# One core, windowed attention and a mixture of experts: the output buffer of a token group as two tiles, with a new set of planner constants

## The chip, the core and the metric

The kernel runs on one core of a Trainium2 chip. The metric is the device time of one execution in microseconds (us). Engines are named as the profile names them: PE (TensorE, matrix products), PEld (its weight loads), DVE (VectorE), ACT (ScalarE), POOL (GpSimd) and SP (SyncE). POOL and SP issue most of the transfers here.

## What is computed

Sliding-window attention with a few sink keys, and then a mixture of four experts on its output. Cut to what matters:

```python
# q, k, v: 4 batches x 8 heads x 768 tokens x 64; n_sink 4, window 128
scores = q @ k.T / sqrt(64)
keep = (pos_k < 4) | ((pos_q - pos_k >= 0) & (pos_q - pos_k < 128))
a = softmax(where(keep, scores, -1e9))
x = (a @ v).transpose(0, 2, 1, 3).reshape(3072, 512)
p = domain_probs / domain_probs.sum(-1)          # 3072 x 4
out = sum(p[:, e:e+1] * (relu(x @ w1[e]) @ w2[e]) for e in range(4))   # w1 512 x 1024, w2 1024 x 512
```

## The kernel before, in words

**Groups and pairs.** Each batch b is cut into three groups g of 256 tokens. A *pair* (b, g) is one such group. Its output is 256 tokens x 512 columns in fp32, held as two halves of 128 tokens. The products of the experts for one pair and one expert are a *unit* (b, g, e).

**Attention.** Scores (L692) and sink scores (L653) go to PSUM, ACT takes the exponential (L717), DVE multiplies by the mask (L711, L726), PE multiplies with the values (L751 for the sinks, L758), DVE takes the reciprocal of the sums (L785), and ACT (L797; in batch 0 DVE, L788) scales into the tile onat. In batch 0, PE turns onat into xT (L816). In batches 1 to 3, a transposing transfer that SP issues does it (L775), and q and k are turned by transposing transfers too (L252, qkT<-qkn). The scores use 64 rows of the PE array at a time (two heads side by side), the sinks 32 columns.

**First layer.** For most units x @ w1 is formed with seven products of half-size blocks instead of eight (P1 to P7, L1158); sums of the token blocks are made on DVE before (L1127), sums of the weight blocks too (L380 to L386), and ACT and DVE combine the products (L1204, L1217, L1211, L1226) and apply Relu and gate (L1191). The other units take the plain product (L1071). The first product of a unit takes two PSUM banks; where the bank for P2 and P6 was not written over its whole width by its last user, one extra matmul of 512 columns (L1166) writes it once.

**Second layer.** For the first two groups of batch 0 it is plain (L1422, results added on DVE by L1432 and L1434 into a tile that both halves share). For the other ten pairs it is again seven products, now over all four experts at once (L1335), in the order of CHAIN: P1, P2, P6, P5, P7, P3, P4. The blocks of the output are C11 and C12 (first 128 tokens, left and right 256 columns) and C21 and C22 (last 128 tokens). After P1, ACT copies the sum to the other bank (L1375). P2 is copied to C11 by ACT, P6 to C12, P5 to C22 and P4 to C21 (all L1397). DVE adds P7 to C22 (L1386) and P3 to C12 (L1381). After P3 the first half is stored (L1383), after P4 and P7 the second (L1324), both by SP.

**The buffer.** Of the ten pairs, the last but one uses two tiles left over from attention. For the others, line 1363 takes one tile osb of both halves with a single buffer (bufs=1). The next tile of that name takes the same memory, and so the first write to it waits for every reader of the one before.

**What sets the order.** The kernel writes its instructions in an order that a planner in the same function decides. It keeps a modelled clock for each engine and picks at each turn what PE does next: a step of attention, a product of a first layer, a product of the second. Work for ACT and DVE is put in a list with a time when it is ready and a time when it is due (`later`), and taken from there by due time (`flush`). SP's and POOL's transfers are written as the planner reaches them. Each engine then works through its own instructions strictly in the order written. The constants at the top (L60 to L100) set due times, preferences and pace: SHARE_OF how much of the expert work of a batch passes while the attention of the next is done, MASK, GATE, GATE0, FORM and TOKEN the slack of DVE's tasks, LOW_PRODUCT and OPEN the rank of products and of opening another unit, HOLDS when two heads' scores are kept for one turn, CHORES how many sums of the second layer may wait at DVE.

Of the kernel before, what the change touches and what calls it, by code (L numbers as in the profile page):

```python
# [11 lines left out]
FP32 = mybir.dt.float32  # L12
# [4 lines left out]
def kernel(  # L17
# [17 lines left out]
    E, Dm, F = moe_w1.shape  # L35
    Ntok, Dout = out.shape

    P = 128
# [19 lines left out]
    ]  # L58

    NGATE = 4  # L60
    FIRST = 1
    START = {0: (1, 0), 1: (0, 2), 2: (0, 0), 3: (1, 0)}
    MIX = 6
    SHARE_OF = (0.9, 0.79, 0.98)
    LEAD = (1.01, 1.0)
    DUE = 1.9
    LOW_PRODUCT = 2.3
    LOW_SECOND = 2.7
    HIGH_PRODUCT = 1.9
    EARLY = -0.01  # L70
    MASK = 4000
    GATE = 1500
    GATE0 = 900
    FORM = 6000
    TOKEN = 5000
    MARGIN = 0
    HOLD = 0
    FULL = 7
    STEP0 = 0.01
    READY = 40  # L80
    WIDE = 2
    OPEN = 2.2
    SOON = 34000
    NEARLY = 2
    ROWED = 24000
    GATED = 38000
# [1 line left out]
    ROWS1 = 1500  # L88
    ONACT = 1
    ONE = 2  # L90
    HOLDS = 1
    MORE = 2
    BOTH = 1
    PAIR = 0
    OVER = 4
    ALONE = 1.3
    BEHIND = 1500
    CHORES = 3
    BIASED = 1
    FAST = tuple(START)  # L100
    BZ = 0
# [122 lines left out]
    mo = ctx.enter_context(tc.tile_pool(name="moe_sb", bufs=2))  # L224
# [224 lines left out]
    def load_gates():  # L449

        while len(gate_sb) < len(mix.order) and (
            len(gate_sb) < (NGATE if t["pe"] > GATED else FIRST) or mix.order[len(gate_sb) - NGATE] in mix.finished
        ):
# [3 lines left out]
    def load_gate(pair, e):  # L457

        x = mo.tile([P, 2, P], FP32, name="gates", tag="gates", bufs=NGATE)
        if FIRST <= len(gate_sb) < NGATE:  # L460
            nc.vector.memset(x[0:1, 0, 0:1], 0.0)
# [474 lines left out]
    out_sb = {}  # L936

    class Mixture:


        def __init__(self):
            self.early = {g: list(range(E)) for g in range(NEARLY)}
            self.open = []
            self.units = []
            for b, g in PAIRS:
                fast = [e for e in range(E) if self.is_fast(b, g, e)]
                slow = [e for e in range(E) if e not in fast]
                if b == 0:
                    fast, slow = list(range(E)), []
                while fast or slow:  # L950
                    for x in (fast, slow):
                        if x:
                            self.units.append((b, g, x.pop(0)))
            self.order = list(self.units)
            self.T, self.T_at, self.fast, self.finished = {}, {}, {}, set()
            self.second, self.live, self.since, self.turn, self.credit = [], 0, 0, 0, 0.0
            self.H, self.H_at, self.H_part = {}, {}, {}
            self.S, self.S_at, self.waiting, self.last = {}, {}, [], []
            self.products = [(b, g, m) for b, g in PAIRS for m in CHAIN]
            self.piece, self.part, self.chores = 0, 0, 0  # L960
            self.at, self.S4_at, self.C22 = {}, {}, {}
            self.done = 0.0
            self.stored, self.homed = [], False
            self.spare, self.lent = [], {}
# [170 lines left out]
        def emit_fast(self, u, m, ready):  # L1135
# [86 lines left out]
            elif m == "P2":  # L1222
                gated(H[:, 0, :, 1], y, 1, end, GATE, slots["Y"])
            elif m == "P7":
# [91 lines left out]
        def emit_product(self):  # L1316
            ready = self.product_ready()
            b, g, m = self.products[0]
            self.done += QF * G
            self.credit = max(self.credit - QF * G, 0.0)  # L1320
            r = (b * NQB + 2 * g) * P

            def store(at, c=slice(0, Dout)):
                nc.sync.dma_start(out=out[r + P:r + 2 * P, c], in_=out_sb[b, g][1][:, c])  # L1324
                sp(at)
            bank = self.bank(b, g, m)
            other = acc[1 - bank][:, 0:G]
            final = (b, g) == PAIRS[-1]
            x = acc[bank][:, 0:G]
            e, k = self.order_of(b, g)[self.piece], self.piece  # L1330
            split = final and m == CHAIN[-1]
            cs = slice(self.part * P, self.part * P + P) if split else slice(0, G)
            y = self.rest if split and self.part else x[:, cs]
            for f in range(QF):
                nc.tensor.matmul(  # L1335
                    y, lhsT=self.operand(b, g, e, m)[:, f], rhs=forms[e][m][:, f, cs],
                    start=(k == 0 and f == 0 and m in (("P1", "P5", "P2") if final else ("P1", "P5"))), stop=(k == E - 1 and f == QF - 1), skip_group_check=True,
                )
            end = pe(QF * (P if split else G), ready, n=QF)
            self.piece = (k + 1) % E  # L1340
            if split and k == E - 1:
                nc.scalar.copy(out=out_sb[b, g][1][:, cs], in_=y)
                store(act(P, end), cs)
                self.part += 1
            if split and self.part < 2:
                return
            if m == CHAIN[-1]:
                if (b, g, e) in self.lent:
                    self.spare.append(self.lent.pop((b, g, e)))
                else:  # L1350
                    self.live -= 1
            if k < E - 1:
                return
            self.products.pop(0)
            if split:
                return
            if m == "P1":
                late = not att.more() and ahead == B - 1
                if late and self.homed:
                    x2 = [sb.tile([P, 2, 4 * P], BF16, name="aT", tag="aT", bufs=4) for _ in range(2)]  # L1360
                    out_sb[b, g] = [i.rearrange("p h w -> p (h w)").bitcast(FP32) for i in x2]
                else:
                    x2 = mo.tile([P, 2, Dout], FP32, name="osb", tag="osb", bufs=1)
                    out_sb[b, g] = [x2[:, i] for i in range(2)]
                self.homed = late and not self.homed
                self.C22[b, g] = join(2, lambda at: store(at))
            o = out_sb[b, g]
            C11, C12, C21, C22 = o[0][:, 0:G], o[0][:, G:], o[1][:, 0:G], o[1][:, G:]
            acc_free[bank], seeded = 1e12, acc_free[1 - bank]
            if m == "P1" and not final:  # L1370
                acc_free[1 - bank] = 1e12

            def run(engine):
                if m == "P1" and not final:
                    nc.scalar.copy(out=other, in_=x)  # L1375
                    acc_free[0] = acc_free[1] = act(G, seeded)
                elif m == "P2" and final:
                    nc.vector.tensor_add(C11, C11, x)
                    acc_free[bank] = dve(G)
                elif m == "P3":  # L1380
                    nc.vector.tensor_add(C12, C12, x)  # L1381
                    acc_free[bank] = at = dve(G)
                    nc.sync.dma_start(out=out[r:r + P, :], in_=o[0])  # L1383
                    sp(at)
                elif m == "P7":
                    nc.vector.tensor_add(C22, C22, x)  # L1386
                    acc_free[bank] = at = dve(G)
                    if final:
                        store(at, slice(G, Dout))
                        i = min((i for i in range(6) if whole[i]), key=lambda i: ring[i])  # L1390
                        self.rest = psum.tile([P, P], FP32, name="rest", tag=f"r{i}", bufs=1)
                        nc.scalar.copy(out=self.rest, in_=x[:, P:G])
                        acc_free[bank] = act(P, end)
                    else:
                        self.C22[b, g](at)
                else:
                    nc.scalar.copy(out={"P1": C11, "P2": C11, "P6": C12, "P5": C22, "P4": C21}[m], in_=x)  # L1397
                    acc_free[bank] = at = act(G)
                    if m == "P4":
                        self.C22[b, g](at)  # L1400
            later("dve" if m in ("P3", "P7") or final and m == "P2" else "act", end, 200, run)
# [7 lines left out]
        def emit_second(self):  # L1409
            ready = self.second_ready()  # L1410
            g, s, e = self.second.pop(0)
            if g not in out_sb:
                out_sb[g] = mo.tile([P, 2, Dout], FP32, name="osb0", tag=f"wide{g}" if g < 2 else "osb", bufs=1)
                if g == 0:
                    gates()
            dst = out_sb[g][:, s]
# [40 lines left out]
    ahead, upto, loaded, wide, rowed = 0, 0.0, 0, 0, 0  # L1457
# [23 lines left out]
    while mix.more() or att.more():  # L1481
        now = t["pe"]

        if not att.more() and ahead == B - 1 and not wide:
            wide = 1
# [27 lines left out]
        if turns and (ahead < 2 or not mix.second) and landed.get(("qk", *turns[0]), 1e12) < now and (turns[0][0] <= ahead or turns[0][0] == ahead + 1 and not att.todo):  # L1513
            x = turns.pop(0)
            turn_nat(*x)
            b = x[0]
# [12 lines left out]
        if ahead + 1 < B and not att.more() and (ahead == 0 or (ahead + 1, 0) in turned_at) and (ahead == 0 or mix.done >= sum(work[:ahead]) * LEAD[ahead - 1]):  # L1529
            ahead += 1  # L1530
            att = Attention(ahead)
            upto = mix.done
        share = (sum(work[:ahead]) - upto) * SHARE_OF[max(ahead - 1, 0)]
        due = ahead == 0 or att.steps * share <= (mix.done - upto) * att.total
# [75 lines left out]
```

## Time and profile before

| | |
|---|---|
| median of 3 runs | 357.3 us (356.98 to 357.76) |
| the profiled execution | 357.25 us, of which the span, first to last instruction, is 355.5 |
| PE busy | 349.7 us, 98% |
| DVE busy | 305.9 us, 86% |
| ACT busy | 165.2 us, 46% |
| POOL busy | 73.6 us, 21% |
| mean granted PE clock | 0.998 |
| transfers | 37.80 MB, mean 106 GB/s |
| L1158, first layer by seven products | 2240 matmuls of 128 columns |
| L1335, second layer by seven products | 1120 matmuls, 1104 of them of 256 columns |

How to read it: a line of the page names engine, line of the kernel and operation, then output<-inputs. On PE, a matmul's row lasts from its start to the modelled end of its results, 219 ns for 128 columns, while the next matmul starts much earlier. So the busy share says when PE had something under way, and the distance between the starts of two matmuls says whether it worked at its full rate. Waits are written as "who waited <- for whom: us in total, times, longest". In a timeline each row is a start, a length and the instructions merged into it, with the idle time before it in brackets. In the table of stages, each engine has its busy time and its number of instructions.

### The profile page before, as it was taken

What the parts mean: (1) busy time and instruction counts of PE and PEld (TensorE: products, weight loads), DVE (VectorE), ACT (ScalarE), POOL (GpSimd) and SP (SyncE); (2) the same over time, 40 slices, a digit from 0 to 9 for tenths busy, and PEclk for the clock granted to TensorE, in tenths of its full rate; (3) what the DMA queues carried; (4) which work ended last, traced back from release to release, by engine and by line L of the source; (5) the groups of instructions that cost most, each with busy time, mean ns of one, the idle gap of its engine ahead of it and who ended that gap; (6) DMA issues with size and microseconds to landing.
All of it is one profiled execution on the core that took longest, in us unless ns stands there. A gap on an engine that the chain in (4) does not pass through costs nothing.

```text
span 355.5 us, 10875 instructions
## 1 busy us (share of the span) xinstructions
PE 349.7 (98%) x4563; PEld 302.4 (85%) x4563; DVE 305.9 (86%) x704; ACT 165.2 (46%) x423; POOL 73.6 (21%) x91
## 2 busy tenths in 40 slices
PE   8999999999999999999999999999999999999996
PEld 3685769656789998998998999899899999999985
DVE  5885999978999999799698998799899899899740
ACT  5863724447884565554542345455464223322111
POOL 8955114230534306010340000000000000000000
PEclk9999999999999999999999999999999999999999
DMA  9999999999999999629999120310210211010011
GB/s 176 178 187 196 222 216 181 170 153 180 150 144 157 177 153 117 78 64 72 160 144 160 46 57 21 77 50 21 77 50 19 52 56 61 31 44 33 1 61 60
DMA packets 120125, 37.80 MB, mean 106 GB/s; under 512 B 101268, under 2 KB 116084, under 8 KB 120076
## 3 DMA queue, kind: packets, MB, share of 16 engines
q0 software_dynamic: 79104, 17.31, 57.7%
q1 hardware_dynamic: 39916, 19.28, 27.5%
q8 instruction: 35, 0.57, 0.7%
q10 hardware_dynamic: 1056, 0.52, 0.5%
q14 instruction: 14, 0.11, 0.1%
HBM read 40.98 MB, written 6.34 MB: 133 GB/s over the span
## 4 chain that ended last, share of the span: by engine, by line
PE 93%; DVE 3%; DMA 2%; ACT 1%; issue 0%; ACTq 0%; DVEq 0%
PE cps L1158 35%; PE acc L1335 33%; PE acc L1422 8%; PE hps L1071 7%; PE sps L692 3%; PE od L758 3%; DMA out_dram<-osb 2%; PE acc L568 1%; PE od L751 1%; DVE onat L788 1%; DVE aT L726 1%; PE tx L816 0%; DVE T L1127 0%; PE tr L589 0%; PE sinks L653 0%; ACT aT L717 0%
## 5 line engine op out<-in xcount | busy, mean ns | idle before, releaser
L1158 PEld LDWEIGHTS <-w 128*128 128x128 bf16 x1280 | 78.7, 98 | 2.9 <-issue 1.3
L1335 PEld LDWEIGHTS <-H 128*128 128x128 bf16 x684 | 63.5, 98 | 7.3 <-issue 1.1
L1191 DVE SCALAR_TENSOR_TENSOR H<-cps,gates 128x512 bf16<-128x512 f32 x96 | 64.1, 678 | 0.1
L1158 PEld LDWEIGHTS <-vf 128*128 128x128 bf16 x960 | 58.4, 98 | 1.0 <-issue 0.3
L717 ACT ACTIVATE aT<-sps 128x512 bf16<-128x512 f32 (+1 forms) x96 | 47.2, 574 | 16.6 <-PE sps L692 16.5
L1335 PE MATMUL acc<-w,H 128*128 128x256 bf16 x408 | 53.9, 273 | 0.0
L1158 PE MATMUL cps<-T,w 128*128 128x128 bf16 x640 | 48.9, 219 | 0.0
L1158 PE MATMUL cps<-xT,w 128*128 128x128 bf16 x640 | 47.6, 219 | 0.0
L1158 PE MATMUL cps<-T,vf 128*128 128x128 bf16 x640 | 46.2, 219 | 0.0
L797 ACT ACTIVATE onat<-od,R 128x64 bf16<-128x64 f32 x144 | 33.2, 320 | 21.2 <-DVE R L785 21.0
L1204 ACT COPY cps<-cps 128x512 f32<-128x512 f32 x40 | 23.2, 579 | 41.1 <-PE cps L1158 22.1
L1397 ACT COPY osb<-acc 128x256 f32<-128x256 f32 x35 | 13.1, 377 | 50.9 <-PE acc L1335 46.1
L1335 PEld LDWEIGHTS <-S 128*128 128x128 bf16 x320 | 30.1, 98 | 4.2 <-issue 1.0
L1071 PE MATMUL hps<-xT,w 128*128 128x256 bf16 x256 | 31.8, 273 | 0.1
L1211 DVE TENSOR_TENSOR cps<-H,cps 128x512 f32<-128x512 f32 x34 | 23.4, 689 | 8.3 <-PE cps L1158 4.3
L1422 PE MATMUL acc<-w,H 128*128 128x512 bf16 x128 | 29.9, 379 | 0.0
L305 POOL DMA_DIRECT2D vx<-in_v_dram x24 | 21.4, 908 | 39.6 <-PE od L758 28.9
L1335 PE MATMUL acc<-wf,H 128*128 128x256 bf16 (+1 forms) x208 | 28.4, 272 | 0.0
L1071 PEld LDWEIGHTS <-w 128*128 128x128 bf16 x256 | 24.2, 98 | 4.5 <-issue 0.7
L1226 DVE TENSOR_TENSOR H<-H,cps 128x512 f32<-128x512 f32 x34 | 23.1, 679 | 2.2 <-PE cps L1158 2.1
L1158 PE MATMUL cps<-xT,vf 128*128 128x128 bf16 x320 | 24.4, 219 | 0.0
L240 POOL DMA_DIRECT2D qkn<-in_q_dram x22 | 19.6, 893 | 22.3 <-DMA qkT<-qkn 14.7
(127 smaller groups left out, 526.7 us busy)
## 6 DMA issues: line engine op xcount, KB each, us to landing
w<-in_moe_w_dram POOLq DMA_DIRECT2D x6, 1024.0 KB, 18.5
out_dram<-osb SPq DMA_DIRECT2D x21, 256.0 KB
gates<-gate_rows SPq DMA_DIRECT2D x40, 128.0 KB
vx<-in_v_dram POOLq DMA_DIRECT2D x24, 128.0 KB, 7.7
qkn<-in_q_dram POOLq DMA_DIRECT2D x22, 128.0 KB, 6.9
qkn<-in_k_dram POOLq DMA_DIRECT2D x22, 128.0 KB, 7.1
w<-in_moe_w_dram POOLq DMA_DIRECT2D x4, 256.0 KB, 7.3
w<-in_moe_w_dram POOLq DMA_DIRECT2D x2, 512.0 KB, 11.0
```

Source lines behind the costliest of these rows:

```text
L240: nc.gpsimd.dma_start(out=both[:, i], in_=src[b, :, tb * P:(tb + 1) * P, :].rearrange("h p d -> p h d"),)
L305: nc.gpsimd.dma_start(out=vx[tb][:, :, 0:D], in_=v[b, :, tb * P:(tb + 1) * P, :].rearrange("h p d -> p h d"),)
L717: nc.scalar.activation(out=a[:, ph], in_=sps[ph][:, 0:w], func=AF.Exp, scale=scale)
L797: nc.scalar.mul(o[:, qi, hp, ph * D:(ph + 1) * D], od[:, qi, ph, 0:D], R[:, qi, ph])
L1071: nc.tensor.matmul(h[:, i].rearrange("p (q n) -> p q n", q=2), lhsT=w1_sb[e][:, db, fb * P:(fb + 1) * P], rhs=xT[b, g][:, :, db], start=(i ...
L1158: nc.tensor.matmul(y[:, f], lhsT=A[:, d, f * P:(f + 1) * P], rhs=T[:, d], start=(m in ("P1", "P5") and f == 0 and d == 0), stop=(d == 1), ...
L1191: nc.vector.scalar_tensor_tensor(out=dst, in0=src, scalar=0.0, in1=gate, op0=ALU.max, op1=ALU.mult)
L1204: nc.scalar.copy(out=tiles["Y"], in_=y)
L1211: nc.vector.tensor_add(tiles["V"], c5, tiles["X"])
L1226: nc.vector.tensor_add(c5, c5, y)
L1335: nc.tensor.matmul(y, lhsT=self.operand(b, g, e, m)[:, f], rhs=forms[e][m][:, f, cs], start=(k == 0 and f == 0 and m in (("P1", "P5", "P2" ...
L1422: nc.tensor.matmul(op, lhsT=H[:, fb // QF, fb % QF, s], rhs=w2_sb[e][:, fb, :], start=(fb == 0), stop=(fb == NFB - 1),)
```

## The change

In `emit_product` the output of a pair becomes two tiles, osb0 for the first 128 tokens and osb1 for the last 128, each with a buffer of its own; copies, additions and stores are the same. The tile of the plain second layer gets a name of its own. Eleven of the planner's constants get other values, and for pair (2, 2) the order of the experts is given by hand, where it was 0, 1, 2, 3. Lines 61 to 1362 of the kernel before move down by one (L692 becomes L693, L1158 L1159, L1335 L1336), later ones (L1383, L1397) keep their numbers.

```diff
     NGATE = 4
+    EXPERTS = {(2, 2): (2, 0, 3, 1)}
...
-    SHARE_OF = (0.9, 0.79, 0.98)
+    SHARE_OF = (0.96, 0.92, 0.94)
...
-    LOW_PRODUCT = 2.3
+    LOW_PRODUCT = 2.7
...
-    MASK = 4000
-    GATE = 1500
-    GATE0 = 900
-    FORM = 6000
-    TOKEN = 5000
+    MASK = 5000
+    GATE = 800
+    GATE0 = 300
+    FORM = 8000
+    TOKEN = 3000
...
-    OPEN = 2.2
-    SOON = 34000
+    OPEN = 2.5
+    SOON = 28000
...
-    HOLDS = 1
+    HOLDS = 2
...
-    CHORES = 3
+    CHORES = 4
...
             for b, g in PAIRS:
-                fast = [e for e in range(E) if self.is_fast(b, g, e)]
+                fast = [e for e in EXPERTS.get((b, g), range(E)) if self.is_fast(b, g, e)]
...
                 else:
-                    x2 = mo.tile([P, 2, Dout], FP32, name="osb", tag="osb", bufs=1)
-                    out_sb[b, g] = [x2[:, i] for i in range(2)]
+                    out_sb[b, g] = [mo.tile([P, Dout], FP32, name=f"osb{i}", tag=f"osb{i}", bufs=1) for i in range(2)]
...
             if g not in out_sb:
-                out_sb[g] = mo.tile([P, 2, Dout], FP32, name="osb0", tag=f"wide{g}" if g < 2 else "osb", bufs=1)
+                out_sb[g] = mo.tile([P, 2, Dout], FP32, name="osbw", tag=f"wide{g}", bufs=1)
```

## The prediction

> **What bounds the kernel now.** I read the page first, then the busy time by stage, then the waits, then PE's timeline at each hole. All times are us of the profiled execution: it took 357.25, its span is 355.5, and 1.7 lies around the span. The median of the runs shown is 357.3, so the two can be used as one.
>
> ```profile
> PE 349.7 (98%) x4563; PEld 302.4 (85%) x4563; DVE 305.9 (86%) x704; ACT 165.2 (46%) x423; POOL 73.6 (21%) x91
> PE 93%; DVE 3%; DMA 2%; ACT 1%; issue 0%; ACTq 0%; DVEq 0%
> ```
>
> PE is busy for all but 5.8 of the span, and 93% of the chain that ended last is PE. So only what changes PE's own stream of work can change the time: matmuls dropped, holes between matmuls closed or opened. The stages say the same, and that DVE stands close behind:
>
> ```profile
> 100.00:125.00 25.00, 25.00 (x370) 22.96 (x367) 24.74 (x63) 14.29 (x42) 8.97 (x11) 1.00 1.89 161
> 175.00:200.00 25.00, 24.66 (x348) 23.04 (x345) 21.57 (x49) 8.93 (x24) 6.13 (x7) 1.00 1.36 128
> 200.00:300.00 100.00, 99.99 (x1466) 93.42 (x1464) 90.91 (x200) 46.33 (x122) 0.00 (x0) 1.00 0.19 52
> ```
>
> The second number of a row is PE's busy time, the fourth (24.74 in the first row) DVE's. Between 25 and 340 us PE shows idle time in one place only, 175 to 200: 0.34. The granted clock is 1.00 throughout. But a busy PE can still have holes, because a matmul's row lasts longer than the distance to the next one. The distance is the measure. In a run without waits it is 55.9 ns for 128 columns (88 matmuls of L1158 in 4.91), 109 ns for 256 columns (48 of L1335 in 5.24), 216 ns for 512 columns (8 of L1422 in 1.73).
>
> The one idle place, in the waits and on PE's timeline:
>
> ```profile
> ACT osb L1397 <- DMA out_dram<-osb: 4.7, 1, 4.7
> PE acc L1335 <- ACT osb L1397: 0.3, 1, 0.3
> ```
>
> ```profile
> 190.54 0.60 PE L1335 MATMUL acc<-qkn,S 128*128 128x256 bf16 x4
> 191.48 0.60 PE L1335 MATMUL acc<-w,S 128*128 128x256 bf16 x4 [0.34 <-ACT osb L1397]
> ```
>
> Four matmuls of 256 columns take 0.44, so the next was due at 190.98 and came at 191.48: a hole of **0.50**, of which the profile calls 0.34 idle. Its cause: the store of the lower half of the pair before (L1324) was issued at 184.00 and took 6.99 on the chain, among the transposes qkT<-qkn (L252) that SP issued around it. ACT's copy of C11 into the single buffer osb waited 4.75 for it, and the bank that PE wanted next was not free.
>
> **The change, part by part.**
>
> *The buffer in two halves.* Nothing is computed or moved differently: 22 stores of the same sizes, the same copies and additions. Only a wait moves. Before, the first write of a pair (C11, after P2) waits for both stores of the pair before, and the later of them is issued only after P4. In seven pairs of the trace, that copy ended up 5.9 to 9.3 behind the issue of that store (126.6 to 132.5, 154.5 to 163.7, 209.3 to 215.2 and so on), and the store took 2.0 to 7.0 to land. After the change the upper half waits for its own store (issued after P3) and the lower half is first written after P5. The same rows give these distances: L1383 to the next copy of C11 at least 13.6, L1324 to the next copy of C22 at least 11.2. In the new order of instructions I count 12.8 to 16. The longest landing, 7.0, is covered with 4 to spare. So the hole of 0.50 goes, and what PE needs next there (S, formed by DVE until 190.2) is there already. Term: **-0.50**; at worst 0, if the wait only comes back elsewhere.
>
> *The refitted order.* The constants change no work, only its order. Counting both orders: PE has the same matmuls but for one; DVE and ACT have the same operations, one Relu and one copy of xT changing sides; SP and POOL issue the same DMAs. Up to 37.6 us PE's order is the same row for row, up to about 97 us nearly so. Three things follow.
>
> (a) L1166, a matmul of 512 columns that only marks a PSUM bank as written, is not needed any more. It lies between matmuls that wait for nothing, so it is worth its distance: **-0.22** (216 ns, L1422's row, same columns).
>
> (b) Scores and sinks (L692, L653) use half or quarter rows of the array, and PE pays for entering and leaving them. Here is a lone one, and a double one:
>
> ```profile
> 153.46 0.60 PE L1335 MATMUL acc<-qkn,H 128*128 128x256 bf16 x4
> 153.99 0.39 PE L692 MATMUL sps<-qkT 64*128 64x128 bf16 x6
> 154.32 0.62 PE L1158 MATMUL cps<-T,w 128*128 128x128 bf16 x8
> ...
> 163.98 0.60 PE L1335 MATMUL acc<-wf,S 128*128 128x256 bf16 x4
> 164.51 0.61 PE L692 MATMUL sps<-qkT 64*128 64x128 bf16 x12
> 165.06 1.05 PE L1335 MATMUL acc<-wf,S 128*128 128x256 bf16 x8
> ```
>
> The first four end their turn 0.44 after they start, so 0.09 is lost on entry; six score matmuls then hold PE for 0.33, twelve for 0.55. Two lone ones cost 2 x 0.42, one double 0.64: each stretch saved is worth 0.20. The trace has 32 such stretches, the new order 31 with the same 280 matmuls: **-0.20**.
>
> (c) The other holes after 37.6 us are small: 0.14 at 80.2, 0.09 at 97.4, 0.07 at 100.8, 0.03 at 149.1, 0.03 at 177.7, 0.06 at 230.9, 0.17 at 278.8; together 0.58. The largest:
>
> ```profile
> 278.21 0.61 PE L1158 MATMUL cps<-xT,vf 128*128 128x128 bf16 x8
> 278.83 0.61 PE L1158 MATMUL cps<-T,w 128*128 128x128 bf16 x8
> ```
>
> Eight should take 0.45 and took 0.62; DVE's addition L1211 had ended at 278.78. Every one is a product or a value that DVE or ACT finished just late, so a new order opens and closes such holes anywhere. I went through PE's waits in the new order and set the rows of the chain behind each (interval of L1191 0.60, L1211 0.60, L711 0.60, L1204 0.48 and so on) against the PE work that covers it. The one at 80.2 stays (same order), one more of about 0.1 opens at some 108 us (a value behind its mask on DVE), and those at 231 and 279 have cover. I take 0.33 left instead of 0.58: **-0.25**. Bounds: all gone, -0.58; or twice as many as now, +0.6, since DVE is the busy engine of nearly every stage and any of some 250 waits may fall short by the 0.03 to 0.17 of these rows.
>
> Beside other work, at nothing: the gates (L463) landed 10 or more before DVE used them, and the transposes qkT for batches 2 and 3 landed 5 or more before PE read them. Those of batch 1 are tighter (one landed at 86.0 for sinks at 86.5), but there the orders of SP, POOL and PE are the same. The Relu and the copy that change sides are 0.60 and 0.29 to 0.37 on engines that PE doesn't wait for there. Head (to the first matmul, 1.40) and tail (last matmul issued at 351.97, then copy and store, 3.55) are as before.
>
> Sum: 357.25 - 0.50 - 0.22 - 0.20 - 0.25 = 356.08, so **356.1**.
>
> A rule of the Trainium skill would price (a) otherwise. "TensorE: Matmul & The Clock Gate", section "Back-to-back issue gap", says that in a real stream of weight loads and matmuls the spacing is about 81 ns at 128 columns and 131 ns at 512. By that (a) would be 0.13 and the sum 356.2; the rows above (55.9 and 216 ns, with a weight load before every matmul) speak against it here. "TensorEngine Tiling (Array Packing)" says that changing the tiling mode drains TensorE; the 0.09 on entry agrees.
>
> **Rivals.**
>
> *The gain is eaten by new holes.* For it: DVE's 24.74 of 25 in 100 to 125, and holes of 0.03 to 0.17 at seven places already. Against it: the chains counted in (c). With the upper bound of (c), 357.25 - 0.92 + 0.6 = 356.9; anything over 356.54 is within 0.2%.
>
> *The buffer's wait stays and SP is the cause.* The store of the upper half now stands on SP behind three transposes L252 that wait for the last scores of a batch. If it too lands late, the 0.50 stays: 356.6. Against: at least 12.8 between issue and need.
>
> *Slower: the xT transpose of batch 1 comes after qkT's.* In the trace SP issues xT<-onat (L775) at 99.68, ahead of three transposes qkT<-qkn (L252, 5.54 for the three, from 105.28). In the new order the three go first, at some 101 us, when the last scores of batch 1 are through. Then xT goes out at about 106.5; L775 took 5.4 to 7.8 to land in this part of the trace, so it lands at 112 to 114.3. DVE's first step on it (forming T, L1127) stands at about 114.5 in the new order, and DVE takes its work strictly in order: behind it queue the additions and gates of the running units and the addition to C22, done at about 115.4, for which PE waits at 117.3: 1.8 to spare. It decides when the landing passes 116.3; from there every us costs one. With the slowest rows (L252 two in 6.98, so three in 10.5; 7.8 to land) it lands at 119.3: 3.0 lost, **359.1**.
>
> *All holes gone:* 357.25 - 0.92 - 0.58 = 355.75.
>
> **How the numbers follow.** About 0.2% (0.7 us) is what a measurement of this kernel can tell from no change, so faster means below 356.54. Forecast (355.9 to 356.5): 0.60. All holes gone or nearly: 0.09, also faster. New holes or the wait staying: 0.20, nearly all within 0.2%. The transpose: 0.11, of which 0.10 ends slower and 0.01 between. So faster 0.69, same 0.21, slower 0.10. The range 355.5 to 357.2 leaves out the transpose case and the worst of the new holes, some 0.15.
>
> **What would show it.** Right: no wait of ACT L1397 on a DMA, no idle PE near 190 us; 31 stretches of L692 and L653 (L693 and L654 in the new numbering); no row of L1167 (L1166 before); a span of 354.3 to 354.4; holes of 0.1 or so near 80 and 108 us. Wrong: idle time of DVE in front of L1128 (L1127 before) near 114 us with DMA xT<-onat as releaser; PE holes behind DVE L1211 or L711 that together exceed 0.6; a wait of osb0 or osb1 on out_dram.

## The result, and the profile after

| | before | after |
|---|---|---|
| median of the timed runs | 357.14 us (356.69 to 357.76, 6 runs) | 355.51 us (355.29 to 355.78, 6 runs) |
| profiled execution, its span | 357.25, 355.5 | 355.59, 353.9 |

The ratio is 0.9954 [0.9941, 0.9967]: 1.63 us less, where 1.2 were forecast (356.1, with 355.9 to 356.5 as the likely band). The profiled executions differ by 1.66, so they can be taken apart for the cause.

The page of after, the same two lines as were shown of before:

```profile
PE 348.1 (98%) x4562; PEld 302.0 (85%) x4562; DVE 306.9 (87%) x704; ACT 164.6 (47%) x423; POOL 73.2 (21%) x91
...
PE 94%; DVE 3%; DMA 2%; POOL 0%; issue 0%; ACT 0%; DVEq 0%
```

One matmul fewer, PE's share of the chain one point up. In the table of stages of after, the stage that had the one idle place, and DVE's busiest one (PE's busy time is the second number of a row, DVE's the fourth):

```profile
100.00:125.00 25.00, 25.00 (x370) 23.28 (x368) 24.34 (x61) 14.37 (x47) 9.63 (x11) 1.00 1.79 147
175.00:200.00 25.00, 25.00 (x361) 23.42 (x359) 23.34 (x56) 10.45 (x32) 7.88 (x9) 1.00 1.42 169
```

The 0.34 of idle time between 175 and 200 us is gone. The waits of after have one row for ACT's copy L1397 into a buffer osb, and it waits for PE, as it should. PE's timeline near 190 us has eight of the matmuls L1336 in one turn of 0.88, without the gap of before:

```profile
ACT osb L1397 <- PE acc L1336: 53.7, 26, 4.3
```

```profile
190.20 0.61 PE L1159 MATMUL cps<-xT,w 128*128 128x128 bf16 x8
190.64 1.04 PE L1336 MATMUL acc<-wf,S 128*128 128x256 bf16 x8
191.52 0.61 PE L1159 MATMUL cps<-T,w 128*128 128x128 bf16 x8
```

Of the small holes, the one at 80.2 is left, as forecast (twelve L759 of 65 columns start 0.61 ahead of the next turn, the 0.14 among them a mask that DVE finished late), and 0.02 at 148.3:

```profile
79.93 0.68 PE L759 MATMUL od<-vx,aT 128*128 128x65 bf16 x12
80.54 0.34 PE L693 MATMUL sps<-qkT 64*128 64x256 bf16 x4
```

**The difference, added up.** I followed PE's starts through both traces. The head is the same (the 341st matmul at 37.15 and 37.17). The hole of the buffer: -0.50. The marking matmul L1166: -0.22. One stretch of scores fewer (31 for 32, as forecast): -0.20. The other holes: 0.58 before, 0.16 after, -0.42. With 0.03 for the head that is -1.31, and the last matmul is issued at 350.66 instead of 351.97, -1.31 too. From there to the end 3.19 instead of 3.55: **-0.36, in a part that was forecast as unchanged.** Together -1.67, the difference of the spans (353.85 and 355.52).

The tail, in what SP does last (L1605, the waits that close the kernel), before and then after:

```profile
L1605 SPq EVENT_SEMAPHORE  x11: 17/28/28, 352.9 to 355.5; - x11
L1605 SPq DRAIN  x3: 7/7/13, 354.7 to 355.0; - x3
```

```profile
L1605 SPq EVENT_SEMAPHORE  x11: 17/28/28, 351.6 to 353.8; - x11
L1605 SPq DRAIN  x3: 7/7/13, 353.0 to 353.3; - x3
```

The same eleven instructions take 2.6 before and 2.2 after. The last store is not the reason: from issue to landing it takes 1.544 and 1.545. The single records of SP's stream tell it (number in the stream, counted from 0, and start in us):

```
before: 205 353.25 | 206 354.08 (last store landed) | 207 354.46 | 208 354.54 | ... | 214 355.46
after:  205 351.21 (last store issued) | 206 351.59 | 207 351.96 | 208 352.04 | ... | 211 352.77 (landed) | ... | 219 353.79
```

In both, SP stands still for 0.35 between records 206 and 207, of which neither waits for anything then. SP has 215 records before and 220 after. So before, record 207 comes after the landing and the pause is paid; after, it comes while SP waits for the landing anyway. Five more waits on SP made the kernel shorter. That is a reading of two traces; whether it holds was asked of the chip.

### The profile page after: what moved, and what is told of

Read it like the earlier page. It is cut to its first block, busy times and chain, and to the rows that moved or that the text cites. A ratio compares the mean times of both kernels' runs of the same rounds, so it can differ in the third digit from the quotient of the medians.

```text
span 353.9 us, 10891 instructions
## 1 busy us (share of the span) xinstructions
PE 348.1 (98%) x4562; PEld 302.0 (85%) x4562; DVE 306.9 (87%) x704; ACT 164.6 (47%) x423; POOL 73.2 (21%) x91
## 4 chain that ended last, share of the span: by engine, by line
PE 94%; DVE 3%; DMA 2%; POOL 0%; issue 0%; ACT 0%; DVEq 0%
PE cps L1159 35%; PE acc L1336 35%; PE acc L1422 8%; PE hps L1072 7%; PE sps L693 3%; PE od L759 3%; DMA vx<-in_v_dram 2%; PE od L752 1%; DVE aT L727 1%; DVE T L1128 1%; DVE onat L789 1%; PE tx L817 1%; PE tr L590 0%; PE sinks L654 0%; PE acc L569 0%; POOL vx L306 0%
## 5 line engine op out<-in xcount | busy, mean ns | idle before, releaser
L1159 PEld LDWEIGHTS <-w 128*128 128x128 bf16 x1280 | 79.1, 98 | 1.5
L1336 PEld LDWEIGHTS <-H 128*128 128x128 bf16 x684 | 63.2, 98 | 7.7 <-issue 1.6
L1159 PEld LDWEIGHTS <-vf 128*128 128x128 bf16 x960 | 58.4, 98 | 1.5 <-issue 0.8
L1336 PE MATMUL acc<-w,H 128*128 128x256 bf16 x408 | 53.9, 273 | 0.0
L1159 PE MATMUL cps<-T,w 128*128 128x128 bf16 x640 | 48.6, 219 | 0.0
L1159 PE MATMUL cps<-xT,w 128*128 128x128 bf16 x640 | 48.3, 219 | 0.0
L1159 PE MATMUL cps<-T,vf 128*128 128x128 bf16 x640 | 46.5, 219 | 0.0
L798 ACT ACTIVATE onat<-od,R 128x64 bf16<-128x64 f32 x144 | 33.4, 325 | 17.9 <-DVE R L786 17.6
L1397 ACT COPY osb<-acc 128x256 f32<-128x256 f32 x35 | 13.2, 376 | 53.8 <-PE acc L1336 53.7
L1336 PEld LDWEIGHTS <-S 128*128 128x128 bf16 x320 | 30.1, 98 | 3.6 <-issue 0.3
L1336 PE MATMUL acc<-wf,H 128*128 128x256 bf16 (+1 forms) x208 | 28.4, 272 | 0.0
L712 DVE TENSOR_TENSOR aT<-aT,mask 128x1024 bf16<-128x1024 bf16 (+1 forms) x36 | 22.7, 636 | 2.1 <-ACT aT L718 2.0
L1159 PE MATMUL cps<-xT,vf 128*128 128x128 bf16 x320 | 24.4, 219 | 0.0
```

What stands on the lines that cost most here:

```text
L712: nc.vector.tensor_mul(a, a, m[:, None, :].to_broadcast([P, 2, w]))
L798: nc.scalar.mul(o[:, qi, hp, ph * D:(ph + 1) * D], od[:, qi, ph, 0:D], R[:, qi, ph])
L1159: nc.tensor.matmul(y[:, f], lhsT=A[:, d, f * P:(f + 1) * P], rhs=T[:, d], start=(m in ("P1", "P5") and f == 0 and d == 0), stop=(d == 1), ...
L1336: nc.tensor.matmul(y, lhsT=self.operand(b, g, e, m)[:, f], rhs=forms[e][m][:, f, cs], start=(k == 0 and f == 0 and m in (("P1", "P5", "P2" ...
```

## The experiments

Theory: the gain is (1) the buffer's hole, which the split takes away, (2) one marking matmul and one stretch, (3) small holes that the order closes, because it gives DVE more lead, and (4) pauses of a sequencer, which lie at fixed counts of its instructions. Rivals: the order alone takes the buffer's hole away and the split is worth nothing (against 1); any other order moves the holes at random (against 3); the pauses hang on what is waited for (against 4). Times are beside runs of the kernel before on the same chip, which had medians of 357.74, 357.36 and 357.64 us beside e0 to e3, e4 to e7, and e8 to e10. e0, e4, e8 and e9 were executed once each, for their profiles: 356.87, 357.33, 360.98 and 365.72 us.

### One part alone

**e1, the two tiles with the old constants.** Of the diff shown, the two edits at osb and nothing else.

> The old constants and the old order of every engine, with osb as two tiles. Theory: the 0.50 hole in front of the matmul at 191.48 was made by the single buffer alone and goes; all other holes stay (0.14 at 80, 0.17 at 279 and so on); the last matmul is issued at 351.5 instead of 351.97, the span is 355.0, the ratio 0.9986. Rival (the store is late on SP whatever the buffer): ACT waits for a store at osb0 or osb1 and the span stays 355.5.

**e2, the new constants with the one tile of before.**

```diff
-                    out_sb[b, g] = [mo.tile([P, Dout], FP32, name=f"osb{i}", tag=f"osb{i}", bufs=1) for i in range(2)]
+                    x2 = mo.tile([P, 2, Dout], FP32, name="osb", tag="osb", bufs=1)
+                    out_sb[b, g] = [x2[:, i] for i in range(2)]
```

> The new constants and order, with osb as one tile of both halves. Theory: the wait comes back, since the first write of a pair again waits for both stores; a hole of up to 0.5 behind a bank that ACT's copy of C11 holds, span 354.2 to 354.4. Rival: in the new order the stores and the next copy of C11 stand 5.9 to 11 apart in PE's work with the late transposes behind the store, so no hole comes, span 353.9 as with both parts, and the split was worth nothing in this order.

**e0, the kernel before once more.**

> The kernel before once more, for how well holes repeat. Theory of fixed holes: the same eight holes within 0.03 each, the one at 191.48 at 0.3 to 0.6 (it hangs on a transfer), last matmul issued at 351.8 to 352.1, 3.55 from there to the end. Rival (holes are chance): other places and other sizes.

Measured: e1 356.59 us, ratio 0.9976 [0.9967, 0.9985]; e2 355.73 us, ratio 0.9945 [0.9933, 0.9958]. e2 has no hole near 190, with a single buffer: its theory fell, the rival held. So **the order alone is worth as much as the whole change (0.9945 and 0.9954, with intervals that overlap), and no gain of the split beside it is seen**. In the old order the split takes the hole away, as e1 shows. e1 gained more than the 0.9986 that was expected; a second hole was gone there, of which more below. Why the order does it, SP's timelines of before, and then of e2, show:

```profile
184.00 0.84 SPq L1324 DMA_DIRECT2D out_dram<-osb  x1
184.94 0.39 SPq L463 DMA_DIRECT2D gates<-gate_rows  x1
185.44 5.71 SPq L252 DMA_TRANSPOSE qkT<-qkn  x2
```

```profile
180.28 0.34 SPq L1325 DMA_DIRECT2D out_dram<-osb  x1
184.37 0.32 SPq L464 DMA_DIRECT2D gates<-gate_rows  x1
185.77 1.99 SPq L253 DMA_TRANSPOSE qkT<-qkn  x1
```

And ACT's copy of C11 that comes after this store, before and then in e2:

```profile
191.06 0.65 ACT L1397 COPY osb<-acc 128x256 f32<-128x256 f32 x2 [4.75 <-DMA out_dram<-osb]
```

```profile
189.88 0.39 ACT L1398 COPY osb<-acc 128x256 f32<-128x256 f32 x1
```

Before, the store is issued at 184.00, needs 6.99 and lands at 190.99, and the copy starts right behind. In e2 it is issued 3.7 earlier and lands at 186.74 (the last of the 16 signals of its landing in the trace), 3.1 ahead of the copy at 189.88. The store itself is hardly faster: 6.46, although the next transpose is issued 5.5 behind it instead of 1.4. So what the order gives is time between the store and the copy; the landing is over before anything waits for it, with the buffer as small as it was. Why the stores land so late here no run shows. Transposes are under way in both, and the transfers together move 166 GB/s between 180 and 191 us before and 167 in e2; between 200 and 300 us of before, where stores land in 2.0 to 3.6, it is 52.

e0 has the same small holes as the first profile at the same places, but only 0.21 at 191 instead of 0.50, less than the 0.3 to 0.6 that was expected; its last matmul is issued at 351.62, also ahead of what was expected. The buffer's hole hangs on a transfer: in the five profiles of the old order with one buffer (before, e0, e3, e4, e10) the store took 6.99 to 7.58 to land and the hole was 0.50, 0.21, 0.38, 0.29 and 0.42. The timed runs go with that: those of the kernel before spread over 1.3 (356.71 to 358.04, 21 runs beside e1 and e2), the 11 of e1 over 0.8, the 5 of e2 over 0.4.

In e1 the hole of 0.17 near 278 was gone too, though neither the order nor a buffer had anything to do there. DVE's stream has three records more by then in e1 (waits of the new buffers), and that led to e4.

### The pauses

**e3, nothing changed but eight loads of 64 bytes on SP at some 325 us** (they go to a tile that nothing reads):

```diff
+            if m == "P2" and (b, g) == PAIRS[-2] and k == E - 1:
+                probe = consts.tile([4, 8, 4], FP32, name="probe")
+                for i in range(8):
+                    nc.sync.dma_start(out=probe[:, i], in_=moe_domain_probs[4 * i:4 * i + 4])
```

> The kernel before with eight loads of 64 bytes on SP at about 325 us (nothing reads them), so that SP has nine instructions more. The end of the span after the last matmul's issue was 3.55 before and 3.19 after the change, and the difference is a pause of 0.3 that SP makes at the same count of its instructions (between its 207th and 208th recorded one) in both. Theory: the pause is bound to that count; nine more instructions put it ahead of the landing of the last store, and the end comes 3.2 behind the last matmul: span 355.2. Rival (the pause is a wait for the landing or chance): 3.5 stays, span 355.5.

Measured: from the last matmul's issue to the end 3.20 instead of 3.55, with the same stores. The closing waits of SP in e3 take 2.2, as after:

```profile
L1609 SPq EVENT_SEMAPHORE  x11: 17/28/28, 352.7 to 354.9; - x11
L1609 SPq DRAIN  x3: 7/7/13, 354.2 to 354.5; - x3
```

The theory holds: the pause goes by the count. All thirteen traces, with 215 to 224 records of SP, say the same: record 207 starts 0.35 to 0.37 behind the end of record 206, whatever the two are. Timed, 357.18 us, ratio 0.999 [0.998, 1.0]; that fits 0.35, but the interval reaches no change.

**e4, three writes of one column on DVE at some 247 us:**

```diff
+            if m == "P6" and (b, g) == (2, 1) and k == E - 1:
+                probe = consts.tile([1, 4], FP32, name="probe")
+                for i in range(3):
+                    nc.vector.memset(probe[:, i:i + 1], 0.0)
```

> The kernel before, with three extra writes of one column on DVE at about 247 us, in an allocation that nothing reads. In four profiles with the old buffer and the old order DVE began L1191 near 278 us some 0.18 later than its last wait and its last instruction allow, and PE had a hole of 0.17 behind it; with the two tiles in the old order the hole was gone, and DVE's stream had a few more instructions there. Theory: DVE makes a pause at a fixed count of its instructions, as SP does at the end of the kernel; three more instructions put the pause ahead of another one, so L1191 begins on time and the hole of 0.17 near 278 us is gone or under 0.05. Rival: the late start hangs on what L1191 waits for, and the hole stays at 0.17. Either way the three writes themselves cost DVE about 0.2 and PE nothing, since DVE has idle time between 247 and 270 us; 357.0 or 357.2.

Measured: the hole near 278 is gone, the other small ones stay to within 0.01. DVE's timeline of before and of e4, at the same two instructions:

```profile
276.70 0.70 DVE L1211 TENSOR_TENSOR cps<-qkT,cps 128x512 f32<-128x512 f32 x1 [1.91 <-ACT cps L1204]
277.48 0.69 DVE L1191 SCALAR_TENSOR_TENSOR qkT<-cps,gates 128x512 bf16<-128x512 f32 x1
```

```profile
276.96 0.69 DVE L1211 TENSOR_TENSOR cps<-qkT,cps 128x512 f32<-128x512 f32 x1 [1.90 <-ACT cps L1204]
277.56 0.68 DVE L1191 SCALAR_TENSOR_TENSOR qkT<-cps,gates 128x512 bf16<-128x512 f32 x1
```

0.78 apart before, 0.60 in e4, after the same idle time behind the same releaser. So one of the seven small holes was no matter of order at all: it was a pause of DVE's sequencer ahead of its record 703 (counted from 0; before, e0 and e3 have it there), met just when DVE had caught up from a wait and had nothing in stock. Three records more, the writes of e4 or the waits of e1, put it into the wait. The time of e4's one execution, 357.33, is above the 357.0 or 357.2 expected: its head was 0.47 longer. What the pause goes with is said in the last section.

**e10, both shifts in the kernel before:**

> The kernel before, its one buffer and its order unchanged, with the three extra writes on DVE at about 247 us and the eight extra loads of 64 bytes on SP at about 325 us: nothing but the counts of the instructions on the two engines. Theory (pauses at fixed counts): the hole of 0.17 near 278 is gone and 3.55 from the last matmul's issue to the end become 3.20; 0.35 + 0.17 = 0.52 less than the kernel before, ratio 0.9985, a third of what the change as a whole brings. Rival: the extra work costs as much as it saves, or the pauses only move to other waits; ratio 0.9995 to 1.0005.

Measured: in its profile, the hole near 278 gone and a tail of 3.22; but in time 357.29 against 357.64 us, ratio 0.9994 [0.9984, 1.0005]. The interval holds both the theory's 0.9985 and no change at all, so the times don't settle it; the parts in the profiles do. The head of e10 was 0.35 longer than that of the kernel before (341st matmul at 37.50), that of e4 0.47, so the sums of single profiles can't replace them.

### Which constants close the small holes

**e5, e6, e7: the two tiles, and a part of the new constants each.** e5 takes SHARE_OF, HOLDS and SOON; e6 MASK, GATE, GATE0, FORM, TOKEN and CHORES; e7 LOW_PRODUCT and OPEN.

> Two tiles, and of the new constants only SHARE_OF, HOLDS and SOON, which set how evenly the units are spread over the span. One L1166 fewer than before (-0.22), 33 stretches of scores and sinks (one more than before, +0.20). Theory (the small holes are places where DVE ends a product or a value just late, and the constants that give DVE more lead close them): the holes that the two tiles alone left, 0.12 near 98, 0.09 near 101, 0.03 near 149, 0.04 near 178 and 0.06 near 231, sum 0.33, stay about as many, 0.2 to 0.5; about 356.8, as with the two tiles alone (356.77). Rival (any other order moves the holes at random, the refit merely kept a good one): anything from 0.1 to 0.8 of holes.

> Two tiles, and of the new constants only MASK, GATE, GATE0, FORM, TOKEN and CHORES, which are how much lead the order gives to what DVE and ACT must finish before PE uses it, and how many small pieces of DVE work may stand between two units. 32 stretches and one L1166 as in the kernel before. Theory: this group closes the small holes, so the 0.33 that the two tiles alone left falls to 0.15 or less and the time by 0.2, to 356.5. Rival (random): holes of 0.1 to 0.8 in other places, 356.5 to 357.2.

> Two tiles, and of the new constants only LOW_PRODUCT and OPEN, which rank the candidates for PE. 32 stretches and one L1166 as in the kernel before. Theory: holes stay about as with the two tiles alone, 0.2 to 0.5, about 356.8. Rival (random): 0.1 to 0.8 of holes, 356.5 to 357.2. The end: SP's pause of 0.35 stays after the landing of the last store, 3.55 from the last matmul's issue to the end, unless the SP instructions differ in number from the two tiles alone; where there are four or more of them more than before it falls beside the wait for the landing, 3.20. The same holds for the other two kernels with part of the constants.

| kernel | holes after 37.8 us, without the buffer's | 341st matmul | last matmul issued | from there to the end | median, ratio |
|---|---|---|---|---|---|
| before | 0.58 | 37.15 | 351.97 | 3.55 | |
| e1, tiles alone | 0.41 | 37.4 | 351.51 | 3.56 | 356.59, 0.9976 |
| e5, pace | 0.84 | 37.16 | 351.76 | 3.21 | 356.55, 0.9984 [0.9973, 0.9995] |
| e6, slack | 0.45 | 37.55 | 351.74 | 3.56 | 356.54, 0.9975 [0.9964, 0.9987] |
| e7, rank | 0.42 | 37.35 | 351.52 | 3.57 | 356.70, 0.9977 [0.9965, 0.9989] |
| e2, all constants | 0.16 | 37.1 | 350.51 | 3.20 | 355.73, 0.9945 [0.9933, 0.9958] |
| after | 0.16 | 37.17 | 350.66 | 3.19 | 355.51, 0.9954 [0.9941, 0.9967] |

The theory that more slack for DVE closes the holes falls: e6 closes those at 97, 101 and 149 and opens one of 0.14 at 269.0 and 0.05 at 187.1. In e6's timelines of PE and DVE, eight matmuls take 0.58 instead of 0.45, and the next turn starts just after the addition L1211 has ended at 268.97, which stood behind a mask in DVE's order:

```profile
268.44 0.61 PE L1158 MATMUL cps<-xT,w 128*128 128x128 bf16 x8
269.02 0.61 PE L1158 MATMUL cps<-T,w 128*128 128x128 bf16 x8
```

```profile
267.68 0.68 DVE L711 TENSOR_TENSOR aT<-aT,mask 128x1024 bf16<-128x1024 bf16 x1
268.28 0.69 DVE L1211 TENSOR_TENSOR cps<-H,cps 128x512 f32<-128x512 f32 x1
```

Without the one at 80.2, 0.27 are left by the tiles alone (the expectation had 0.33) and 0.31 in e6. e6's time, 356.54, is the one that the theory gave, but e1 and e5 have it too. e5 opens 0.26 at 119.3 and five others; it has the short tail and no marking matmul, and the holes and one more stretch take that back. So holes of 0.03 to 0.3 went and came with each order tried, and none of the three groups carries the gain: each with the tiles is worth what the tiles alone are worth within the intervals, and only all the constants together gave an order with 0.16. Pairs of groups were not run, and the order of the experts given by hand for (2, 2) is in none of the three: that it carries part of the gain is not ruled out. Why this order has so few holes was not found. SP's records bear the pause out once more: e5 has 219 of them and a tail of 3.21, e6 and e7 have 215 and 3.56 and 3.57.

### The prices of a stretch and of a marking matmul

**e8, the kernel after with each head's scores by themselves:**

```diff
-            return self.b >= PAIR and len(self.scored) <= MORE and len(self.todo) > 1 and self.todo[0][::3] == self.todo[1][::3] and self.todo[0][0] == "scores"
+            return False and len(self.todo) > 1 and self.todo[0][::3] == self.todo[1][::3] and self.todo[0][0] == "scores"
```

> The kernel after, with a unit's scores never put together with those of the next one: 43 stretches of scores and sinks instead of 31, with the same 280 matmuls in them. It asks for the price of a stretch, 0.20 each in the forecast (0.42 for a lone one of six, 0.64 for a double of twelve). Theory: last matmul's issue 2.4 later, plus what holes the other order opens; 2.2 to 3.2. Rival: the loss on entry and on leaving lies beside other waits or weight loads, and a stretch saved is worth half of that or less; 0 to 1.2.

Measured: the last matmul is issued 5.41 later, outside what was expected. Of that, some 3.0 are new holes, the largest 0.80 at 103.2, where the profile has PE wait for ACT's L798. The rest, some 2.4 over 12 stretches, is **about 0.20 for each**: the price holds, the time did not, since this order too opened holes. A lone stretch in PE's timeline of e8 (the four L1336 should end their turn 0.44 after they start, and six scores take 0.33):

```profile
153.86 0.60 PE L1336 MATMUL acc<-qkn,H 128*128 128x256 bf16 x4
154.39 0.39 PE L693 MATMUL sps<-qkT 64*128 64x128 bf16 x6
154.72 0.62 PE L1159 MATMUL cps<-T,w 128*128 128x128 bf16 x8
```

**e9, the kernel after with the marking matmul ahead of all 40 first products** (`if m == "P1" and unset:` becomes `if m == "P1":`):

> The kernel after, with the marking matmul of 512 columns (L1167) ahead of all 40 products of the kind that can have it, instead of none: 40 more matmuls of 512 columns whose result is overwritten by the next one. It asks for the price of (a) by itself. Theory: each costs its distance, 216 ns, 40 of them 8.6, less the 0.16 of holes that DVE gains cover for: last matmul's issue 8.4 to 8.7 later. Rival, by the Trainium skill (TensorE: Matmul & The Clock Gate, section Back-to-back issue gap), 131 ns each: 5.2. A third: a marking matmul ahead of a wait costs nothing, and some are; the more the kernel's waits cover, the less, 4 to 8.

Measured: the last matmul is issued 10.05 later, more than was expected. Holes take 1.23 of that and the head 0.21; 8.6 are left for 40, 0.215 each. The single distances say it without a sum: 38 of the 40 are 215 or 216 ns (the other two run into a wait), as here from 183.58 to 183.80:

```profile
183.58 0.38 PE L1167 MATMUL cps<-w 128*128 128x512 bf16 x1
183.80 0.61 PE L1159 MATMUL cps<-T,w 128*128 128x128 bf16 x8
```

The 131 ns of the Trainium skill ("TensorE: Matmul & The Clock Gate", section "Back-to-back issue gap") do not hold in this stream, with a weight load before every matmul: forty would have been 5.2. Expected was a little less than the gross price, since DVE gains cover; instead 1.23 of new holes came with the longer PE work, half of them at 338.0, where PE waits for ACT's copy L1375.

## Why the forecast fell short: the tail, and the small holes

The sum was 356.08; measured were 355.51, and 355.59 in the profiled execution. That is below the band of 355.9 to 356.5, and even below the 355.75 that the forecast gave for no small hole left at all. The step that failed is the tail: it was put at nothing, with "Head (to the first matmul, 1.40) and tail (last matmul issued at 351.97, then copy and store, 3.55) are as before" as the only reason. That 355.51 still lies above the 355.5 at which the stated range begins, by 0.01, is luck: the range was made from the holes, not from the tail.

- *The tail: put at nothing, measured -0.36.* The matmul, the copies and the store do take the same time. SP's pause was in the trace of before, 354.08 to 354.46 with nothing to wait for, and the forecast read the tail as one number of 3.55 instead of asking what it is made of and which of it goes by counts of instructions, which the change shifts. "So only what changes PE's own stream of work can change the time" left no room for it, though 3.55 of the span lie behind the issue of the last matmul.
- *(c), the small holes: mis-sized, -0.25 forecast, -0.42 measured.* The one at 80.2 stayed as said. The one forecast "at some 108 us" did not come, and those at 97.4, 100.8, 177.7 and 230.9 closed. The hole at 278.8 was priced as a value that DVE finished late, which it was; that DVE was late by a pause that three more records move was not seen. The orders of e1, e2, e5, e6, e7 and after had sums of such holes between 0.16 and 0.84, so one figure for an order that has not run says little.
- *The buffer, -0.50: right in the sum, half right in cause.* The hole went. But "after the change the upper half waits for its own store" was not what it took: with the new order the one buffer waits for nothing (e2). The forecast had named the true cause, the late landing, and then looked only at the distance that the split adds, not at how much earlier than the copy the new order issues the store. And 0.50 is the hole of the one execution that was profiled, the largest of five; their mean is 0.36. A store's landing of at most 7.0 was counted on; in e2 one took 9.32 (issued at 118.98), which nothing waited for.
- *(a), the marking matmul, -0.22: right.* 215 to 216 ns each in e9.
- *(b), the stretch, -0.20: right.* 31 stretches, and about 0.20 for each in e8. (The sinks use 32 columns of the array, not a part of its rows, as (b) has it; the price is the same.)

The two misses, -0.17 and -0.36, are the whole distance: 356.08 - 0.53 = 355.55, and the profiled execution took 355.59. The wait on SP in the slower rival (the transpose xT after those of qkT) didn't cost anything: in after, xT was issued at 108.02 and landed at 111.60, and DVE, busy until then, began on it at 114.76. The new holes of the first rival did not come here, but they did in e8 and e9 (some 3.0 and 1.23), so it was right to give it a chance.

## What to carry to other kernels

Before a wait on a buffer is answered with another buffer, look at why the release is late: a store that lands late can be issued further ahead of the next write by the order, and here the buffer was then worth nothing. Take the head and the tail of a kernel apart record by record too, with what each instruction waits for; where one starts late with nothing to wait for, a change that only adds or drops instructions can gain or lose it. A forecast can price what is counted (matmuls, stretches) closely, while the holes of a rearranged order have to be given as a range, here 0.2 to 0.8 for most orders and up to 3.

## What the hardware showed that was not expected

- SP stands still for 0.35 between its records 206 and 207 (counted from 0), whatever these are, and for 0.44 to 0.46 ahead of record 79 in twelve of the thirteen traces (in e8 a longer wait lies there): 128 apart. DVE had one of 0.40 ahead of its record 703 in before, e0 and e3. They cost nothing where the engine waits anyway, and up to 0.36 of the time at the kernel's end. The traces hold instruction packets of two sizes, here those of after (35 with 0.57 MB, 16 KB each, and 14 with 0.11 MB, 8 KB each):

```profile
q8 instruction: 35, 0.57, 0.6%
...
q14 instruction: 14, 0.11, 0.1%
```

  The Trainium skill ("Runtime: NRT & Kernel Launch", section "Instruction fetch mechanics") tells of fetches in blocks of 256 instructions that are hidden behind the issue of instructions. The pauses seen here are 128 apart and were not hidden. They go with the packets of 8 KB: in all thirteen traces one starts 0.62 to 0.93 after SP's record 207, and in before, e0 and e3 one starts 0.67 to 0.96 after DVE's record 703, near 278 us; in e4 and e10, which have no pause there, no such packet lies between 271 and 329 us, and one more stands near 270. That the sequencer pauses in order to ask for the next block is argued from this; no run shows it by itself.
- A store of 256 KB took 6.99 to land before and 6.46 in e2 while transposes were under way around it, where others of the same line took 2.0; and the hole behind it was 0.21 in one execution of a program and 0.50 in another.
- The 341st matmul starts between 37.1 and 37.6 in the profiles, though PE's order is the same up to there: the head alone varies by as much as all the small holes of the kernel are worth.
